# Two kept weight chunks in spare PSUM columns, read back in quarters; five ring slots, 48 resident chunks and 32-wide transposes

## The chip, the cores and the metric

One core of a Trainium2 chip runs the whole kernel. The metric is the time of one execution in device microseconds; the number that counts is the median of the runs. The profile is one execution, recorded by the hardware; "TensorE" and PE are the same engine, as are VectorE and DVE, ScalarE and ACT, GpSimd and POOL, SyncE and SP.

## The reference

Two independent parts, their outputs set side by side. Part A is a long convolution by FFT (2048 steps, 1024 channels) with a short shift filter. Part B, where the change lies, is an attention with a recurrent memory over 64 segments of 32 steps:

```python
def _A_ref(q, k, v, shift_k, ssm_k, ssm_D):
    ...                                   # kv = shifted k * v
    y = irfft2(rfft2(kv_pad) * rfft2(kf_pad))[:, :S]
    y = y + kv * ssm_D[None, None, :]
    return q * y

def _B_ref(x, mem0, Wq, Wk, Wv, Wo, seg_len):      # 32 heads of 128, M = 8 memory rows
    mem = mem0
    for s in range(n_seg):                          # 64 segments
        h = jnp.concatenate([mem, x[:, s*seg_len:(s+1)*seg_len]], axis=1)   # 40 rows
        q, k, v = h @ Wq, h @ Wk, h @ Wv            # einsum 'btd,dhe->bhte'
        scores = jnp.where(mask, q @ k^T * scale, -1e9)
        o = softmax(scores) @ v
        o = jnp.einsum('bhte,hed->btd', o, Wo)
        mem = o[:, :M, :]                           # feeds the next segment
        outs.append(o[:, M:, :])
return jnp.concatenate([a, b], axis=-1)
```

Each segment needs all four weight matrices, and its memory rows come out of the segment before.

## The kernel before

The first part of the program (up to about 392 us) computes part A and, between its stages, the keys, queries and values of the last 8 steps of every segment, which need no memory; they go to DRAM (REC for keys, queries and x, VBD for values). Up to 445 us the last of these values are computed (L765), while weights for the recurrence are placed. Then come the 64 segments, in an order written out by hand.

The weights of part B are cut into 64 chunks of 128 x 2048 bf16 (512 KB). A chunk is named by its position 0 to 63 in the order of use: 0 to 7 keys of head group 0 (the projection k0), 8 to 15 q0, 16 to 23 k1, 24 to 31 q1, 32 to 39 and 40 to 47 the values (pv0, pv1), 48 to 63 the output projection. 47 chunks stay in SBUF (tiles Wres, Wmid, Wmore, Wlate, pw). The 17 of `STREAM` are read from a DRAM copy (WS) in every segment by SP (L724) into a ring of six slots (`wring0` to `wring5`): when a chunk has been used, `done` frees its slot and `fetch` issues the next load into it. SP issues in program order, so a load that waits for its slot holds up those behind it. The slot `wring2` comes free only in segment 0, because the value stores to VBD (L768) leave from its memory.

Two of the 17 are kept in spare PSUM columns after segment 0 (`KEPT`, copied by `keep`). "A" lies in the bank of OTp and is copied back to SBUF by four DVE copies, `quarter` (L817), into the buffers tagged rot and QT; the output projection uses it in four pieces. Of "B", five eighths are kept; `fetch` loads the rest (192 KB, L721) into a ring slot and moves the kept part into the same slot by two DVE copies (`move`, L800). So a segment has 15.4 loads.

A projection (`Proj.run`, L918) takes 8 chunks; of each chunk four matmuls, 32 columns of weights wide, work side by side on four column tiles of the array. ScalarE casts the sum to SBUF (`evac`, L927, buffer rot), four 128-wide transposes (L933) turn it, and DVE or ScalarE copies the result (the first keys: L1027 on DVE; the first queries: L1031 on DVE). Between a cast and its transposes stands half a projection of other work. Scores are L939 and L942, the weighted values L980 and L984, the output projection L1002 (64-wide, two side by side). At the end of a segment ScalarE casts the result to Y (L1078, buffer PT), POOL stores Y to the output (L1080, two DMAs), and `fill_mem` transposes Y (L862, two pairs) to put the 8 memory rows into the next segment's input (L863): the first pair before any projection, the second after four chunks of k0.

The pools release a buffer when everything that read it is done, DMAs included. The tag PT is shared by Y and by PT, the softmax result; QT by the first output rows and the second queries; rot by all casts.

Of the kernel before, what the change touches and what calls it, by code (L numbers as in the profile page):

```python
# [18 lines left out]
NEG = -1.0e9  # L19


STREAM = (0, 5, 10, 15, 21, 26, 31, 36, 41, 46, 49, 52, 54, 57, 60, 61, 63)
KEPT = {14: "A", 4: "B"}
K0_ORDER = (0, 1, 4, 5, 2, 3, 6, 7)
N2, N3 = 12, 19
WO_COPY = 29
Q_LOAD = (10, 13, 16, 19)
X_LOAD = 1
RING = 6
LATE_SLOT = 4  # L30

PITCH = 2048
SCRATCH = 1024
# [383 lines left out]
def b_kernel(ctx: ExitStack, tc, x, mem0, Wq, Wk, Wv, Wo, outb, n_seg, run_a):  # L417
    nc = tc.nc
# [19 lines left out]
    streamed = set()  # L438
# [21 lines left out]
    def stream_src(ch):  # L460
        return WS[ring_order.index(ch), :, 0:2048]
# [233 lines left out]
    def more(i):  # L695
# [7 lines left out]
    kept = {order_s[i]: name for i, name in KEPT.items()}  # L703
    at_hand = {}
    loads = [(s, ch) for s in range(n_seg) for ch in order_s
             if s == 0 and ch not in v_temp[2:] or s > 0 and kept.get(ch) != "A"]
    live = {}
    now = [0]
    free = [4, 5, 0, 1, 3]
# [6 lines left out]
    def fetch():  # L716
        if loads:
            s, ch = loads.pop(0)
            live[s, ch] = k, t = slot()
            if s > 0 and ch in kept:  # L720
                nc.sync.dma_start(t[:, 0:768], stream_src(ch)[:, 0:768])  # L721
                move(kept[ch], t, True)
            else:
                nc.sync.dma_start(t[:], stream_src(ch))  # L724

    def place(ch, ap):
        res[ch] = ap
# [11 lines left out]
    with c0p:  # L739
        temps = dict(zip(v_temp, homes_v))  # L740
        wv = [group(2, 0, temps), None]
        for _ in rest:
            store()
        wv[1] = group(2, 1, temps)
        for i, ch in enumerate(v_temp):
            if i >= 2:
                home = (lambda i=i: more(i)) if i < len(v_temp) - 2 else (lambda k=i - len(v_temp) + 4: pw(k))
                at_hand[ch] = (wv[ch[2]][ch[1]], home)
        while stores:
            store()  # L750
        with tc.issue_after(got[-1].ins):
            for _ in range(2):
                fetch()
        n_k = len(own[0, 0])
        late = late[n_k:-1] + late[4:n_k] + late[:4] + late[-1:]
        for g in range(2):
            ws = wv[g]
            if g == 0:
                vsts = slot16([128, 4, 4, 512], BF, "vst")
            for tb in range(4):  # L760
                vst = vsts[:, tb] if g == 0 else pair()[:].rearrange("p (c w) -> p c w", c=4)
                for c in range(4):
                    ps = ps0.tile([128, 512], F32, tag="ps0", name="vb_ps")
                    for kc in range(8):
                        nc.tensor.matmul(ps[:], lhsT=xbt(kc)[:, 16 * tb:16 * tb + 16, :].rearrange("p s t -> p (s t)"),  # L765
                                         rhs=ws[kc][:, c * 512:(c + 1) * 512], start=(kc == 0), stop=(kc == 7))
                    evac(vst[:, c, :], ps[:])
                nc.scalar.dma_start(  # L768
                    VBD[16 * tb:16 * tb + 16, :, :, :, g * 128:(g + 1) * 128].rearrange("s t c i e -> (s t) (c i) e"),
                    vst.rearrange("p c (i e) -> p (c i) e", i=4))  # L770
            if g == 0:
                with tc.issue_after(got[-1].ins):
                    place_late(4, stage_home)
                    for i in [*range(len(v_temp) - 2, n_more), *range(len(v_temp) - 2)]:
                        place_late(1, lambda: more(i))
                    place_late(1, lambda: pw(2))
                    place_late(4, stage_home)
        assert len(late) == len(at_hand)

    one = ctx.enter_context(tc.tile_pool(name="b_one", bufs=1, side="right", reuse_waits="tile"))  # L780
# [11 lines left out]
    homes = {"B": [(OTi[:, :, 416:512], slice(384, 768)), (tpi[:, 1, :], slice(768, 1024))]}  # L792

    def move(name, t, back):
        for p, cols in homes[name]:
            w = t[:].bitcast(I32)[:, cols]
            if len(p.shape) == 3:
                w = w.rearrange("p (b x) -> p b x", b=4)
            src, dst = (p, w) if back else (w, p)
            nc.vector.tensor_scalar(out=dst, in0=src, scalar1=0, scalar2=None, op0=ALU.bitwise_or)  # L800

    def quarter_cols(q):
        return [1024 * (q // 2) + 512 * dh + 256 * (q % 2) for dh in range(2)]
# [1 line left out]
    def keep(ch):  # L805
        t = live[0, ch][1]
        if kept[ch] == "A":
            w = t[:].bitcast(I32).rearrange("p (hh dh f x) -> p hh f dh x", hh=2, dh=2, f=2)
            for q in range(4):
                nc.vector.tensor_scalar(out=OTi[:, q, 160:416].rearrange("p (dh x) -> p dh x", dh=2),  # L810
                                        in0=w[:, q // 2, q % 2], scalar1=0, scalar2=None, op0=ALU.bitwise_or)
        else:
            move(kept[ch], t, False)

    def quarter(q):
        t = one.tile([128, 512], BF, tag=("rot", "QT")[q % 2], name="quarter")
        nc.vector.tensor_scalar(out=t[:].bitcast(I32), in0=OTi[:, q, 160:416], scalar1=0, scalar2=None,  # L817
                                op0=ALU.bitwise_or)
# [15 lines left out]
    def done(ch):  # L834
        if now[0] == 0 and ch in at_hand:
            place_late(1, at_hand[ch][1])
        elif ch in streamed and (now[0] == 0 or kept.get(ch) != "A"):
# [3 lines left out]
            i = order_s.index(ch)  # L841
            if now[0] == 0 and i == LATE_SLOT:
                free.append(2)
                fetch()
            fetch()

    P_pad = one.tile([128, 5, 64], BF, name="P_pad")
# [18 lines left out]

    with tc.manual_schedule():
        for _ in range(RING - 3):
            fetch()
        load_x(0)  # L870
        Y = one.tile([128, 512], BF, tag="PT", name="Y0")
# [12 lines left out]
        for s in range(n_seg):  # L884
# [19 lines left out]
            class Proj:  # L904


                def __init__(self, m, g):
                    self.m, self.g, self.kc = m, g, 0
                    self.acc = ps_acc.tile([128, 512], F32, tag="acc", name="acc")

                def run(self, n=8):
                    for n_kc in range(self.kc, self.kc + n):
                        kc = K0_ORDER[n_kc] if (self.m, self.g) == (0, 0) else n_kc
                        ch = (self.m, kc, self.g)
                        w = pieces(ch)
                        for c in range(4):
                            for x, y, r in columns(w, 512 * c, 512 * c + 512):
                                nc.tensor.matmul(self.acc[32 * c:32 * c + 32, x - 512 * c:y - 512 * c],  # L918
                                                 lhsT=hT[:, kc, :], rhs=r, start=(n_kc == 0 and x == 512 * c),
                                                 stop=(n_kc == 7), tile_position=(0, 32 * c))  # L920
                        done(ch)
                    self.kc += n
                    return self

# [5 lines left out]
            def transposes(sb):  # L930
                tp = tps[:, 0, :]
                for i in range(4):
                    nc.tensor.transpose(tp[:, i * 128:(i + 1) * 128], sb[:, i * 128:(i + 1) * 128], ident[:])  # L933
                return tp.rearrange("p (i c r) -> p i c r", i=4, c=4)

            def scores(g, QT, KT):
# [89 lines left out]
            last_queries(0)  # L1026
            nc.vector.tensor_copy(KT0[:, :, :, 0:32], transposes(k0))  # L1027
# [125 lines left out]
```

## Time and profile before

| | |
|---|---|
| median of 3 runs | 1904.04 us (1904.03 to 1904.1) |
| profiled execution, time | 1907.36 us |
| profiled execution, span of the core | 1905.6 us |
| mean granted TensorE clock | 0.982 (1.00 in the segments) |
| bytes by DMA | 678 MB, mean 356 GB/s |
| loads of L724 | 961, and 63 partial ones of L721 |
| start of segment 1 and segment 63 | 475.81 and 1879.10 us |

The page gives for every engine its busy time in the span; the slices show when. In the segments each engine's work repeats every 22.5 us, so one segment read closely stands for all. A busy TensorE in this view can still stand still for a short time between matmuls; that is read in the timeline, from one start to the next.

### The profile page before, as it was taken

What the parts mean: (1) busy time and instruction counts of PE and PEld (TensorE: products, weight loads), DVE (VectorE), ACT (ScalarE), POOL (GpSimd) and SP (SyncE); (2) the same over time, 40 slices, a digit from 0 to 9 for tenths busy, and PEclk for the clock granted to TensorE, in tenths of its full rate; (3) what the DMA queues carried; (4) which work ended last, traced back from release to release, by engine and by line L of the source; (5) the groups of instructions that cost most, each with busy time, mean ns of one, the idle gap of its engine ahead of it and who ended that gap; (6) DMA issues with size and microseconds to landing.
All of it is one profiled execution on the core that took longest, in us unless ns stands there. A gap on an engine that the chain in (4) does not pass through costs nothing.

```text
span 1905.6 us, 62245 instructions
## 1 busy us (share of the span) xinstructions
PE 1749.0 (92%) x26353; PEld 831.1 (44%) x26353; DVE 853.8 (45%) x2812; ACT 674.8 (35%) x1195; POOL 342.8 (18%) x1014
## 2 busy tenths in 40 slices
PE   6989986778999999999999999999999999999998
PEld 3433322333444444444444444444444444444444
DVE  9927863202344444444444444444443444444443
ACT  6945640112333333333333333333333333333333
POOL 4003341000121111111121111111111111111111
PEclk9999998989999999999999999999999999999999
DMA  9989889998999999999999999999999999999998
GB/s 338 351 302 329 291 271 333 327 284 277 349 373 374 373 378 373 377 372 373 373 373 378 373 376 372 370 372 372 379 374 369 371 378 374 375 373 371 372 379 311
DMA packets 251211, 678.00 MB, mean 356 GB/s; under 512 B 74850, under 2 KB 82930, under 8 KB 250932
## 3 DMA queue, kind: packets, MB, share of 16 engines
q1 hardware_dynamic: 178692, 604.26, 85.0%
q0 software_dynamic: 17488, 46.70, 7.0%
q10 hardware_dynamic: 54752, 23.07, 4.5%
q8 instruction: 206, 3.38, 0.7%
q14 instruction: 73, 0.60, 0.1%
HBM read 618.35 MB, written 59.24 MB: 356 GB/s over the span
## 4 chain that ended last, share of the span: by engine, by line
PE 80%; DMA 7%; DVE 5%; issue 4%; ACT 2%; POOL 0%; ACTq 0%; SPq 0%; DVEq 0%; POOLq 0%
PE acc L918 38%; PE yacc L1002 22%; PE kb_ps L625 5%; PE tps L933 4%; DMA wring<-WS 3%; PE vb_ps L765 3%; DMA REC<-stage 2%; PE OTp L980 1%; ACT s_sb L243 1%; DVE rec L863 1%; PE SB L942 1%; PE tps L862 1%; PE s_ps L241 1%; DMA REC<-xt 1%; PE SB L939 1%
## 5 line engine op out<-in xcount | busy, mean ns | idle before, releaser
L918 PEld LDWEIGHTS <-rec 128*32 128x32 bf16 x12288 | 283.6, 96 | 300.2 <-DVE rec L863 60.7
L927 ACT CAST qkv_sb<-acc 128x512 bf16<-128x512 f32 x384 | 224.7, 585 | 480.0 <-PE acc L918 287.9
L1002 PEld LDWEIGHTS <-OT 128*64 128x64 bf16 x4348 | 255.1, 109 | 195.3 <-ACT OT L992 27.6
L918 PE MATMUL acc<-wring,rec 128*32 128x512 bf16 x2556 | 252.7, 382 | 22.8 <-DVE rec L863 19.1
L918 PE MATMUL acc<-Wres,rec 128*32 128x512 bf16 x3328 | 249.4, 380 | 0.6 <-issue 0.6
L1002 PE MATMUL yacc<-wring,OT 128*64 128x512 bf16 (+1 forms) x1540 | 235.9, 380 | 5.0 <-DMA wring<-WS 4.9
L918 PE MATMUL acc<-Wmid,rec 128*32 128x512 bf16 x3072 | 234.4, 382 | 0.0
L1002 PE MATMUL yacc<-Wmore,OT 128*64 128x512 bf16 (+1 forms) x1280 | 185.4, 381 | 0.0
L817 DVE TENSOR_SCALAR quarter<-OTp 128x256 int32<-128x256 int32 x252 | 101.1, 422 | 187.6 <-ACT OT L992 149.3
L1080 POOL DMA_DIRECT2D out_dram<-Y x128 | 63.7, 502 | 484.5 <-ACT Y L1078 484.2
L918 PE MATMUL acc<-pw,rec 128*32 128x512 bf16 x1796 | 144.8, 382 | 0.1
L1078 ACT CAST Y<-yacc 128x256 bf16<-128x256 f32 x128 | 41.4, 375 | 274.5 <-PE yacc L1002 274.5
L992 ACT CAST OT<-OTp 128x640 bf16<-128x640 f32 x128 | 88.6, 692 | 129.7 <-PE OTp L984 129.0
L918 PE MATMUL acc<-Wlate,rec 128*32 128x512 bf16 x1280 | 104.0, 384 | 17.1 <-DVE rec L863 17.1
L948 DVE TENSOR_REDUCE mx<-SB 128x5 f32<-128x200 f32 x128 | 47.1, 368 | 153.4 <-PE SB L942 153.3
L856 POOL DMA_DIRECT2D rec<-REC x64 | 36.2, 566 | 405.0 <-PE acc L918 372.1
L1002 PE MATMUL yacc<-Wlate,OT 128*64 128x512 bf16 x768 | 105.7, 383 | 0.2 <-ACT OT L992 0.2
L933 PEld LDWEIGHTS <-qkv_sb 128*128 128x128 bf16 x1024 | 57.8, 97 | 109.5 <-ACT qkv_sb L927 108.0
L933 PE MATMUL tps<-ident,qkv_sb 128*128 128x128 bf16 x1024 | 101.6, 222 | 0.4 <-ACT qkv_sb L927 0.3
L893 POOL COPY KT<-rec 128x128 bf16<-128x128 bf16 x128 | 38.2, 298 | 329.4 <-PE SB L942 324.2
L863 DVE COPY rec<-tps 128x32 bf16<-128x32 bf16 x128 | 22.3, 175 | 165.1 <-PE tps L862 115.8
L1027 DVE COPY KT<-tps 128x512 bf16<-128x512 bf16 x64 | 27.1, 424 | 152.2 <-PE tps L933 152.2
(215 smaller groups left out, 2392.9 us busy)
## 6 DMA issues: line engine op xcount, KB each, us to landing
wring<-WS SPq DMA_DIRECT2D x961, 512.0 KB, 6.0
rec<-REC POOLq DMA_DIRECT2D x64, 192.0 KB, 5.8
wring<-WS SPq DMA_DIRECT2D x63, 192.0 KB
SK<-s_sb SPq DMA_DIRECT2D x16, 512.0 KB, 4.8
SU<-s_sb SPq DMA_DIRECT2D x16, 512.0 KB, 4.9
Kg<-SK SPq DMA_DIRECT2D x32, 256.0 KB, 4.2
Ug<-SU SPq DMA_DIRECT2D x32, 256.0 KB, 5.7
REC<-stage ACTq DMA_DIRECT2D x16, 512.0 KB, 10.9
```

The lines of the kernel that those rows point to most:

```text
L625: nc.tensor.matmul(ps[:], lhsT=ws[kc][:, hl * 128:(hl + 1) * 128], rhs=xbt(kc).rearrange("p s t -> p (s t)"), start=(kc == 0), stop=(kc == 7))
L765: nc.tensor.matmul(ps[:], lhsT=xbt(kc)[:, 16 * tb:16 * tb + 16, :].rearrange("p s t -> p (s t)"), rhs=ws[kc][:, c * 512:(c + 1) * 512], st ...
L817: nc.vector.tensor_scalar(out=t[:].bitcast(I32), in0=OTi[:, q, 160:416], scalar1=0, scalar2=None, op0=ALU.bitwise_or)
L863: nc.vector.tensor_copy(hT.rearrange("p (dh j) t -> p dh j t", dh=2)[:, :, 2 * half:2 * half + 2, 0:NM], tp.rearrange("p (j dh r) -> p dh ...
L918: nc.tensor.matmul(self.acc[32 * c:32 * c + 32, x - 512 * c:y - 512 * c], lhsT=hT[:, kc, :], rhs=r, start=(n_kc == 0 and x == 512 * c), st ...
L927: nc.scalar.copy(sb[:], self.acc[:])
L933: nc.tensor.transpose(tp[:, i * 128:(i + 1) * 128], sb[:, i * 128:(i + 1) * 128], ident[:])
L948: nc.vector.tensor_reduce(out=mx[:], in_=S, op=ALU.max, axis=AX.X)
L992: nc.scalar.copy(OT[:], o_view)
L1002: nc.tensor.matmul(yacc[64 * dh:64 * dh + m, x - o:y - o], lhsT=lhsT, rhs=r, start=(h == 0 and x == o), stop=(h >= 30), tile_position=(0, ...
L1078: nc.scalar.copy(Y[:, 256 * half:256 * half + 256], yacc[:, 256 * half:256 * half + 256])
L1080: nc.gpsimd.dma_start(bass.AP(outb.tensor, outb.offset + SEG * s * 2048 + 512 * dh, [[2048, 32], [1, 512]]), Y[64 * dh + NM:64 * dh + 40, :])
```

## The change

`STREAM` is a new list of 16 positions; 48 chunks are resident, the 48th in `wring2`, and the ring has five slots. Both kept chunks, A (now position 61) and B (now position 20, in k1), stay in PSUM whole (the last eighth of B in an SBUF tile `B_rest`), and neither is loaded after segment 0: 14 loads a segment. B is used like A in four quarters, `quarter_b`, each copied by DVE into a work buffer (PT, QT, PT, rot) and multiplied inside k1, out of its turn in the sum. Only three chunks and two quarters now stand between q0's cast and its transposes, where four chunks stood. The copy of the first queries goes from DVE to ScalarE. All 128 x 128 transposes of the segments become four of 32 columns each, on four column tiles (`turn_tile`).

```diff
-STREAM = (0, 5, 10, 15, 21, 26, 31, 36, 41, 46, 49, 52, 54, 57, 60, 61, 63)
+STREAM = (1, 7, 13, 18, 20, 24, 30, 35, 41, 46, 49, 52, 55, 59, 61, 62)
 KEPT = {14: "A", 4: "B"}
-RING = 6
-LATE_SLOT = 4
+RING = 5
...
-             if s == 0 and ch not in v_temp[2:] or s > 0 and kept.get(ch) != "A"]
+             if s == 0 and ch not in v_temp[2:] or s > 0 and ch not in kept]
...
-            if s > 0 and ch in kept:
-                nc.sync.dma_start(t[:, 0:768], stream_src(ch)[:, 0:768])
-                move(kept[ch], t, True)
-            else:
-                nc.sync.dma_start(t[:], stream_src(ch))
+            nc.sync.dma_start(t[:], stream_src(ch))
...
+        place_late(1, lambda: base.tile([128, 2048], BF, tag="wring2", name="Wring"))
...
+    B_rest = one.tile([128, 4, 32], I32, name="B_rest")
+    B_homes = [tpi[:, 1, :].rearrange("p (c x) -> p c x", c=4),
+               SB[:].bitcast(I32)[:, 200:456].rearrange("p (c x) -> p c x", c=4),
+               OTi[:, :, 416:480], OTi[:, :, 480:512]]
+
+    def bits(dst, src):
+        nc.vector.tensor_scalar(out=dst, in0=src, scalar1=0, scalar2=None, op0=ALU.bitwise_or)
+
+    def quarter_b(q, tag):
+        n = 64 if q < 3 else 32
+        t = one.tile([128, 4, 2 * n], BF, tag=tag, name="quarter_b")
+        bits(t[:].bitcast(I32), B_homes[q])
+        w = [(512 * c + 128 * q, 512 * c + 128 * q + 2 * n, t[:, c, :]) for c in range(4)]
+        if q == 3:
+            w += [(512 * c + 448, 512 * c + 512, B_rest[:].bitcast(BF)[:, c, :]) for c in range(4)]
+        return w
...
+    def turn_tile(dst, src):
+        for e in range(0, 128, 32):
+            nc.tensor.matmul(dst[e:e + 32, :], lhsT=src[:, e:e + 32], rhs=ident[:], start=True, stop=True,
+                             is_transpose=True, tile_position=(0, e))
...
-            nc.tensor.transpose(tp[:, j * 128:(j + 1) * 128], Y[:, j * 128:(j + 1) * 128], ident[:])
+            turn_tile(tp[:, j * 128:(j + 1) * 128], Y[:, j * 128:(j + 1) * 128])
...
-        for _ in range(RING - 3):
+        for _ in range(RING - 2):
             fetch()
...
+                def add(self, kc, w, start=False, stop=False):
+                    for c in range(4):
+                        for x, y, r in columns(w, 512 * c, 512 * c + 512):
+                            nc.tensor.matmul(self.acc[32 * c:32 * c + 32, x - 512 * c:y - 512 * c],
+                                             lhsT=hT[:, kc, :], rhs=r, start=start and x == 512 * c,
+                                             stop=stop, tile_position=(0, 32 * c))
...
-                    nc.tensor.transpose(tp[:, i * 128:(i + 1) * 128], sb[:, i * 128:(i + 1) * 128], ident[:])
+                    turn_tile(tp[:, i * 128:(i + 1) * 128], sb[:, i * 128:(i + 1) * 128])
...
-            k1 = Proj(0, 1).run(4)
+            k1 = Proj(0, 1)
+            if s > 0:
+                kb = [ch[1] for ch in kept if kept[ch] == "B"][0]
+                b0, b1 = quarter_b(0, "PT"), quarter_b(1, "QT")
+                k1.run(1)
+                k1.add(kb, b0)
+                b2 = quarter_b(2, "PT")
+                k1.run(2)
+                k1.add(kb, b1)
+            else:
+                k1.run(4)
             QT0 = one.tile([128, 4, 4, 32], BF, tag="QT", name="QT")
-            nc.vector.tensor_copy(QT0[:], transposes(q0))
-            k1 = k1.run(4).evac()
+            nc.scalar.copy(QT0[:], transposes(q0))
+            if s > 0:
+                b3 = quarter_b(3, "rot")
+                k1.run(3)
+                k1.add(kb, b2)
+                k1.add(kb, b3)
+            k1 = k1.run(8 - k1.kc).evac()
```

More of the change, by code (lines that the diff above doesn't have):

```diff
@@ L791, in b_kernel @@
     OTi, tpi = OTp[:].bitcast(I32), tps[:].bitcast(I32)
[L792 to L800, printed above, removed]
+    B_rest = one.tile([128, 4, 32], I32, name="B_rest")
[12 more added lines that the diff above has]
+        return w
     def quarter_cols(q):
@@ L809, in keep @@
             for q in range(4):
-                nc.vector.tensor_scalar(out=OTi[:, q, 160:416].rearrange("p (dh x) -> p dh x", dh=2),
-                                        in0=w[:, q // 2, q % 2], scalar1=0, scalar2=None, op0=ALU.bitwise_or)
-        else:
-            move(kept[ch], t, False)
+                bits(OTi[:, q, 160:416].rearrange("p (dh x) -> p dh x", dh=2), w[:, q // 2, q % 2])
+        else:
+            w = t[:].bitcast(I32).rearrange("p (c f x) -> p f c x", c=4, f=4)
+            for q in range(3):
+                bits(B_homes[q], w[:, q])
+            bits(B_homes[3], w[:, 3, :, 0:32])
+            bits(B_rest[:], w[:, 3, :, 32:64])
     def quarter(q):
         t = one.tile([128, 512], BF, tag=("rot", "QT")[q % 2], name="quarter")
-        nc.vector.tensor_scalar(out=t[:].bitcast(I32), in0=OTi[:, q, 160:416], scalar1=0, scalar2=None,
-                                op0=ALU.bitwise_or)
+        bits(t[:].bitcast(I32), OTi[:, q, 160:416])
         return [(o, o + 256, t[:, 256 * dh:256 * dh + 256]) for dh, o in enumerate(quarter_cols(q))]
@@ L836, in done @@
             place_late(1, at_hand[ch][1])
-        elif ch in streamed and (now[0] == 0 or kept.get(ch) != "A"):
+        elif ch in streamed and (now[0] == 0 or ch not in kept):
             if now[0] == 0 and ch in kept:
@@ L840, in done @@
             free.append(live.pop((now[0], ch))[0])
[L841 to L844, printed above, removed]
             fetch()
@@ L914, in run @@
                         ch = (self.m, kc, self.g)
[L915 to L921, printed above, removed]
+                        if s == 0 or ch not in kept:
+                            self.add(kc, pieces(ch), n_kc == 0, n_kc == 7)
+                            done(ch)
                     self.kc += n
```

## The prediction

> **What bounds the kernel now.** I read the page's busy rows first, then the windows of single segments, then the chain, then the timeline around one transpose, then the landings of the output store. The page, busy us of each engine:
>
> ```profile
> PE 1749.0 (92%) x26353; PEld 831.1 (44%) x26353; DVE 853.8 (45%) x2812; ACT 674.8 (35%) x1195; POOL 342.8 (18%) x1014
> ```
>
> The windows (stretch, its length, busy us of each engine with its count, granted clock, DMA share, GB/s):
>
> ```profile
> 800.00:822.52 22.52, 21.46 (x392) 10.64 (x388) 9.51 (x36) 7.45 (x15) 3.87 (x14) 1.00 1.01 381
> 450.00:455.00 5.00, 5.00 (x112) 2.54 (x108) 2.59 (x7) 1.83 (x3) 0.90 (x5) 1.00 1.05 408
> ```
>
> A segment of the recurrence takes 22.52 us at full clock; TensorE (PE) is busy for 21.46 of them, and the DMA share reads 1.01. So there are two candidates for the bound. The chain decides. From 475.81 us to the end its longest pieces are these, and there are only five of this kind:
>
> ```profile
> 945.32 7.86 DMA wring<-WS
> 1171.45 7.56 DMA wring<-WS
> ...
> 1757.82 7.56 DMA wring<-WS
> ```
>
> Segment starts (the first L862 transpose of each) lie 22.51 to 22.52 us apart in most segments. The 62 intervals from 475.81 to 1879.10 sum to 1403.3 us, 7.0 more than 62 x 22.52: 2.8 in the first, 4.2 in all others. So TensorE's own order is the bound, and late loads cost 7 us altogether. Also, 1.01 is not the end of the queue: 450 to 455 us shows 408 GB/s where a segment needs 381. Cutting traffic alone is worth 7 us at most; the rest must come from TensorE.
>
> TensorE's order at one transpose (start, us, engine, line, operation, out<-in, count):
>
> ```profile
> 820.16 0.58 ACT L927 CAST qkv_sb<-acc 128x512 bf16<-128x512 f32 x1 [3.06 <-issue]
> 820.54 0.39 PE L918 MATMUL acc<-Wmid,rec 128*32 128x512 bf16 x4
> 820.86 0.40 PE L933 MATMUL tps<-ident,qkv_sb 128*128 128x128 bf16 x4
> 821.19 0.61 PE L918 MATMUL acc<-Wmid,rec 128*32 128x512 bf16 x8
> 821.29 0.42 DVE L1027 COPY KT<-tps 128x512 bf16<-128x512 bf16 x1 [2.33 <-PE tps L933]
> 821.63 0.39 PE L918 MATMUL acc<-Wlate,rec 128*32 128x512 bf16 x4
> ```
>
> Four 32-wide projection matmuls run side by side; a chunk takes 0.216 us (821.63 to the next at 821.85). The chunk of 820.54 therefore leaves the array at 820.755, but the first transpose starts at 820.86: 0.105 idle. The four transposes start 0.056 apart (820.86, 820.93, 820.98, 821.04 in the trace), so they end at 821.095, and the next chunk starts at 821.19: 0.09 idle. The block takes 0.43 us for 0.22 of streaming. Between 32-wide projections and 32-wide scores (L939) there is no such gap.
>
> **The change, part by part.**
>
> *32-wide transposes.* Each 128-wide transpose becomes four 32-wide ones side by side, the shape of the projections. If they overlap like projections, streaming stays 4 x 0.056 and both gaps go: 0.215 less for each of the four L933 blocks. But the first gap also hid a wait on ScalarE. From a projection's last matmul start to the end of its cast is 0.494 + 0.58 (821.85 to 822.34, then 0.58), and 0.06 to reach PE: 1.13 us. With four chunks between, PE arrives after 0.216 x 5 = 1.08, so 0.05 of the gain is lost at k0 and q1 (0.16 each is left). At k1 the scores lie between: all 0.215. At q0 the change puts only three chunks and two quarters between: 0.216 + 3 x 0.216 + 2 x 0.056 = 0.98, so PE waits 0.16 and 0.05 is left. The second L862 pair loses its 0.11 gap; the first waits for Y anyway: 0. Sum: 0.16 + 0.05 + 0.215 + 0.16 + 0.11 = 0.695 us a segment.
>
> *Quarters of chunk B on PE.* Four groups of 128 columns and the last split in two of 64, instead of one chunk of 512: 4 x 0.056 against 0.216, so 0.01. The nearest rows agree on both sides: the 256-wide quarter pairs of A take 0.11 (813.73 to 813.84), the 40-wide score groups start 0.025 apart. A rule speaks against this: the Trainium skill, TensorEngine Tiling (Array Packing), section Instruction Overhead, gives every matmul about 60 cycles and warns against tiling what is already small. Taken as serial cost, an estimate from that page is 16 more matmuls x 0.025 us (60 columns' worth of a 0.216 us chunk) = 0.4 us a segment, and the sum would be 25 us worse; the score groups show 0.006 per matmul.
>
> *Copies on VectorE (DVE).* Removed: two copies back (0.56 + 0.41, L800) and the Q copy (0.42), which goes to ScalarE at 0.58 behind q0's cast and before k1's; scores come 1.2 us after it, 1.05 is needed: 0. Added: three copies of 0.42 like L817 and one half as wide, about 0.28. The first starts when the K copy ends, 0.84 after the k0 transposes start, is done at 1.27 and wanted at 0.224 + 0.864 + 0.216 = 1.30: just in time. The last one overwrites the buffer that the q0 transposes read: 0.42 + 0.28 + 0.06 = 0.76 after their start, wanted at 0.71: 0.05.
>
> *The new wait.* The first copy goes into the buffer tagged PT, last used by Y, so it waits until both output stores of the segment before have landed. Behind it on DVE stand the other three copies and the softmax; PE waits for all of them. Today PT's next writer comes about 9 us later. The stores are issued 0.52 and 1.02 us after the segment starts (at 816.87), as the timeline has it:
>
> ```profile
> 817.39 1.00 POOL L1080 DMA_DIRECT2D out_dram<-Y  x2 [7.34 <-ACT Y L1078]
> ```
>
> The store's own view, from 700 to 1800 us and for the last segment (duration of the issue in ns; time from issue to landing):
>
> ```profile
> L1080 POOL DMA_DIRECT2D out_dram<-Y x98: 496/502/509, 704.8 to 1790.0; - x98
> ...
> DMA to landing us min/median/max: 4.2/4.8/5.8
> ...
> L1080 POOL DMA_DIRECT2D out_dram<-Y x2: 496/496/496, 1902.1 to 1902.6; - x2
> ...
> DMA to landing us min/median/max: 1.7/1.7/1.8
> ```
>
> Call L the time from the first issue to the second landing: 5.3 today, 2.2 in the last segment, where no loads run. B's first quarter is wanted 5.2 us after the segment starts; landing, copy and two hand-overs end at 0.52 + L + 0.53. The wait is L - 4.15, of which 0.1 replaces the wait at q0. Bounds: 0 at L = 2.2, 1.05 at 5.3. What L follows is the loads in flight at the issue: counted from the DMA packets, 3.1 today and none at the end. After the change the slots freed shortly before are those of positions 59 and 62, at -2.2 and -0.9 us, and no load is cut short; with the 1.2 us from issue to first packet and 1.25 per load that is 1.5 to 1.8 in flight. L grew by 3.1 us for 3.1 loads, 1 us each, so it should be 3.7 to 4.0, nearer to the last segment's end than to today's; with the scatter of 0.5 above I take 0.03. A rule would settle it: the Trainium skill, DMA: Bandwidth & Descriptors, section Queues, rings and completion order, says that an engine round-robins between rings packet by packet; then a store would hardly feel the loads and the wait would be 0. The rows above, 1.7 against 4.8, contradict it.
>
> *Fourteen loads, five slots.* 15.4 chunks of 524 KB fall to 14: 8.37 to 7.65 MB a segment, 349 GB/s at 21.9 us. Loads land after a median of 6.0 us (4.8 to 7.9). From slot free to next use there are now 7.1 to 8.6 us; by the new positions 6.2 to 8.3, the tightest being 52, 49 and 35. These are issued where loads landed after 5.5 to 5.9. Cost 0.02; of today's 7 us, 5 come back.
>
> *Segment 0.* The 48th chunk goes to wring2, whose last user is the VBD store of L768, issued at 445.8. It is needed as the fifth chunk, at 447.0. That store takes 15.0 us beside ten loads; with five, I count about 9, then 3.5 for the chunk: PE stops until about 458. SyncE (SP) holds the next loads behind it, but all five slots are full by then. Today segment 0 takes 30.0 us from 445.8, with 7.5 of waits at 463 to 475. New: 1.2 + 11 + 20.8 + 1 = 34: 4 us more (0 to 9). The stages before: one copy to WS less, no other step on the chain, 0 +- 2.
>
> **Sum.** A segment: -0.695 + 0.01 + 0.05 + 0.03 + 0.02 = -0.585, so 21.93 us. Times 63: -36.9. Stalls -5, segment 0 +4: -37.9. The profiled execution took 1907.36 us (span 1905.6, 1.8 around it): 1869.5. The median of the runs, 1904.04, lies 3.3 below it: 1866. Own range: gains of 0.45 to 0.72 a segment and the bounds of segment 0 and the stalls give 1852 to 1882.
>
> **Rivals.**
> 1. *The store holds B's first quarter.* If L stays at 5.3, each segment pays 1.05 more: 22.95 us, +27 for 63, +4 in segment 0, -5 of stalls: 1930. It turns slower from L of about 4.85. For: 4.2 to 5.8 in every segment today. Against: half the loads in flight, and a waiting PE lets the queue empty. 0.17.
> 2. *Five slots starve.* If loads at the tight places took 7.7, PE would wait 1.3 us a segment: about 1948. Against: 9% fewer bytes. 0.08.
> 3. *Transposes do not overlap.* Sixteen in a row take 0.9 us instead of 0.22: +2.7 for four blocks, +0.6 for the fills: about 2075. Against: the projections overlap in this shape. 0.08.
> 4. *Nothing to gain*: other waits take up the gaps, 1897 to 1910: 0.07.
>
> **Numbers.** Forecast 0.60. The range 1850 to 1930 leaves out rivals 2 in part and 3 and the tails. Faster by over 0.2% (which is about what a measurement can tell): the forecast, some of 1, 2 and 4: 0.73; same 0.05; slower 0.22.
>
> **What would show it.** Right: segments 21.8 to 22.0 apart; L918 to L862/L933 without a gap; a wait of about 0.15 at q0's transposes; quarter_b's first copy waiting little or not on out_dram; one stop of about 11 us on Wring in segment 0. Wrong: DVE idle on out_dram for 1 us a segment, PE on wring, or 0.05 between single transposes.

## The result, and the profile after

The changed kernel takes 1968.1 us (median, 1960.52 to 1976.29) against 1904.07 us for the kernel before on the same chip: a ratio of 1.0331, 95% interval 1.0286 to 1.0376. It is slower; the forecast was 1866, faster. The profiled execution took 1969.65 us, with a span of 1967.8.

The page of the changed kernel, its busy row, the queue that brings instructions (packets, MB, share), and the chain by engine:

```profile
PE 1719.1 (87%) x31169; PEld 872.0 (44%) x31201; DVE 864.5 (44%) x2877; ACT 709.0 (36%) x1259; POOL 344.9 (18%) x1013
...
q8 instruction: 244, 4.00, 0.8%
...
PE 67%; DMA 18%; DVE 4%; ACT 4%; issue 4%; POOL 2%; ACTq 1%; DVEq 0%; another core or an unknown queue 0%; POOLq 0%; SPq 0%
```

TensorE (PE) has less to do, 1719 us instead of 1749, although it has more matmuls. But it no longer works through: 87% of the span instead of 92%. The windows show it in one stretch of 22.5 us:

```profile
1000.00:1022.50 22.50, 19.78 (x436) 10.67 (x436) 9.49 (x36) 7.98 (x15) 2.71 (x12) 1.00 0.88 314
```

PE is busy for 19.78 us of it, the DMA share is 0.88. So neither TensorE's work nor the bandwidth sets the time, and the clock is full (1.00). Over 62 segments a segment takes 23.52 us on average, 22.63 before, and 21.93 in the forecast. The waits of PE between 500 and 1840 us (who waited, for whom: us in total, times, longest) name the two things in between:

```profile
PE acc L920 <- DVE quarter_b L794: 53.2, 57, 2.2
...
PE acc L920 <- issue: 7.2, 11, 1.3
PE OTp L989 <- issue: 3.7, 6, 1.2
```

The first row is the wait for B's first quarter, in nearly every segment. The rows with "issue" are stops in which PE waited for no semaphore; with the smaller ones they sum to 14.5 us here. In the same view of the kernel before all of them come to 0.6 us. The timeline shows the one stop of segment 0, and then one segment in which the wait is long:

```profile
458.52 0.62 PE L920 MATMUL acc<-Wring,rec 128*32 128x512 bf16 x4 [12.06 <-DMA Wring<-in_B_Wk_dram]
...
998.67 1.02 POOL L1104 DMA_DIRECT2D out_dram<-Y  x2 [7.33 <-ACT Y L1102]
...
1002.01 0.41 PE L862 MATMUL tps<-ident,qkv_sb 128*32 128x128 bf16 x16
1002.24 0.39 PE L920 MATMUL acc<-Wmid,rec 128*32 128x512 bf16 x4
...
1004.97 0.42 DVE L794 TENSOR_SCALAR quarter_b<-tps 128x256 int32<-128x256 int32 x1 [2.08 <-DMA out_dram<-Y]
...
1005.45 0.24 PE L920 MATMUL acc<-quarter_b,rec 128*32 128x128 bf16 x4 [1.95 <-DVE quarter_b L794]
```

Sixteen narrow transposes start at 1002.01, and the next chunk at 1002.24: 0.23 us for the block that took 0.33 and a gap of 0.1 before it. That part of the change works. Then DVE stands 2.08 us until the output store has landed, and PE 1.95 us until the copy is there. The store's own view, from 500 to 1900 us:

```profile
DVE quarter_b L794: 49.9, 48
...
DMA to landing us min/median/max: 3.5/4.7/5.9
```

48 copies waited for it. A store lands after 4.7 us, 4.8 before: the relief that the forecast counted on isn't there.

### The profile page after: what moved, and what is told of

It is laid out like the page before. It is cut to its first block, busy times and chain, and to the rows that moved or that the text cites. A ratio compares the mean times of both kernels' runs of the same rounds, so it can differ in the third digit from the quotient of the medians.

```text
span 1967.8 us, 71785 instructions
## 1 busy us (share of the span) xinstructions
PE 1719.1 (87%) x31169; PEld 872.0 (44%) x31201; DVE 864.5 (44%) x2877; ACT 709.0 (36%) x1259; POOL 344.9 (18%) x1013
## 4 chain that ended last, share of the span: by engine, by line
PE 67%; DMA 18%; DVE 4%; ACT 4%; issue 4%; POOL 2%; ACTq 1%; DVEq 0%; another core or an unknown queue 0%; POOLq 0%; SPq 0%
PE acc L920 26%; PE yacc L1011 23%; DMA out_dram<-Y 13%; PE kb_ps L624 4%; PE tps L862 3%; PE vb_ps L760 3%; DMA REC<-stage 2%; PE OTp L989 1%; DVE quarter_b L794 1%; POOL out_dram L1104 1%; ACT Y L1102 1%; ACT s_sb L242 1%; PE SB L951 1%; PE s_ps L240 1%; PE SB L948 1%
## 5 line engine op out<-in xcount | busy, mean ns | idle before, releaser
L920 PEld LDWEIGHTS <-rec 128*32 128x32 bf16 x13296 | 321.7, 96 | 368.3 <-issue 108.7
L920 PE MATMUL acc<-Wres,rec 128*32 128x512 bf16 x3328 | 254.9, 380 | 5.9 <-issue 5.1
L920 PE MATMUL acc<-Wmid,rec 128*32 128x512 bf16 x3072 | 247.7, 381 | 0.0
L920 PE MATMUL acc<-wring,rec 128*32 128x512 bf16 x2304 | 232.6, 381 | 1.5 <-issue 1.4
L1011 PE MATMUL yacc<-Wmore,OT 128*64 128x512 bf16 x1536 | 210.5, 381 | 0.1
L1011 PE MATMUL yacc<-wring,OT 128*64 128x512 bf16 (+1 forms) x1284 | 196.9, 379 | 3.1 <-DMA wring<-WS 2.7
L920 PE MATMUL acc<-Wlate,rec 128*32 128x512 bf16 x1280 | 115.3, 385 | 22.1 <-DVE rec L869 21.2
L920 PE MATMUL acc<-quarter_b,rec 128*32 128x128 bf16 x1008 | 58.1, 216 | 58.6 <-DVE quarter_b L794 58.4
L862 PE MATMUL tps<-ident,qkv_sb 128*32 128x128 bf16 x4096 | 106.1, 220 | 1.9 <-issue 1.7
L862 PEld LDWEIGHTS <-qkv_sb 128*32 128x32 bf16 x4096 | 71.9, 96 | 65.0 <-ACT qkv_sb L936 45.4
```

The source lines that it names most:

```text
L862: nc.tensor.matmul(dst[e:e + 32, :], lhsT=src[:, e:e + 32], rhs=ident[:], start=True, stop=True, is_transpose=True, tile_position=(0, e))
L1011: nc.tensor.matmul(yacc[64 * dh:64 * dh + m, x - o:y - o], lhsT=lhsT, rhs=r, start=(h == 0 and x == o), stop=(h >= 30), tile_position=(0, ...
```

## The experiments

The theory after this result had two costs that add up: the wait for the store, about 1.0 us a segment (the forecast's first rival), and the stops without a semaphore, about 0.5. The other candidates were the narrow transposes themselves, the five slots and the quarters. Each time is compared with the kernel before on the same chip.

**Another buffer for the first quarter.**

```
-                b0, b1 = quarter_b(0, "PT"), quarter_b(1, "QT")
+                b0, b1 = quarter_b(0, "E"), quarter_b(1, "QT")
```

> The changed kernel, but the first quarter of chunk B is copied into the buffer tagged E (softmax scratch, idle then) and not into PT, so that it does not wait for the output store of Y. Theory: two losses, the wait for the store (first quarter multiplied 6.3 us after the segment starts, where 5.2 was expected; about 1.0 us a segment) and PE stops of about 0.5 us a segment between instructions that wait for no semaphore. Taking away the first gives 63 x 0.95 = 60 us: 1905 to 1920, with segments 22.3 to 22.8 us apart, and the PE stops stay. Rival (five slots and a later DMA are the bound, the wait for the store only shows it): the wait moves to wring, 1945 or more.

Measured: 1961.73 us, ratio 1.0292 [1.0264, 1.032]. The wait is all but gone from the trace (2.6 us in 7 waits): the first quarter's matmul comes 5.17 us after the segment's start (6.3 on average with the store). But the time hardly moved (1905 to 1920 was expected), because the stops without a semaphore took its place. PE's waits, 500 to 1840 us:

```profile
PE tps L862 <- issue: 19.4, 21, 1.7
PE acc L920 <- issue: 15.7, 18, 1.7
PE SB L951 <- issue: 7.3, 9, 1.6
```

All "issue" rows together are 51.4 us here, against 14.5 with the wait in place. The rival's 1945 or more holds as a number only, since PE waits 0.3 us in all for a ring load. The stops had been named before this run; that they would grow when the wait goes was in no theory.

**The transposes 128 wide again, all else changed.**

```
-        for e in range(0, 128, 32):
-            nc.tensor.matmul(dst[e:e + 32, :], lhsT=src[:, e:e + 32], ... tile_position=(0, e))
+        nc.tensor.transpose(dst, src, ident[:])
```

> The changed kernel with 128-wide transposes again, all else as changed. Theory (the PE stops come from the supply of PE instructions, of which the 32-wide transposes add 120 a segment): the stops of 0.5 us a segment go, the two gaps of 0.2 us behind B's first quarter come back, those ahead of it lie in the wait for the store: 1950 to 1970. Rival (the number of instructions does not matter, the gaps do): about 0.4 us a segment more, 1990 or above.

Measured: 1959.95 us, 1.0285 [1.0259, 1.031]. This is what the theory expected: the stops without a semaphore are gone (0.7 us in all), the wait for the quarter stays (32 us in 46 waits over the run). The interval overlaps that of the whole change (1.0286 to 1.0376), so the narrow transposes bring the change nothing that shows.

**The narrow transposes alone, in the kernel before** (`turn_tile` of the change in place of both transposes).

> The kernel before with the 32-wide transposes alone. By the prediction's term, 0.695 us a segment less: 63 x 0.695 = 44 us, 1860, if nothing else comes up. Theory (instruction supply): 96 pairs more a segment give some PE stops, 0.2 to 0.4 us a segment, so 1870 to 1885. Rival (the transposes gain nothing, or the loads become the bound at 8.4 MB a segment): 1895 or above, with PE waiting on wring.

Measured: 1954.06 us, 1.0259 [1.0231, 1.0287]: the part that was to bring the gain makes the kernel slower by itself. The theory had expected far less of the stops (1870 to 1885); the rival's 1895 or above came, but not its cause, since PE waits 0.5 us in all for the ring. PE's waits, 500 to 1840 us:

```profile
PE acc L923 <- issue: 24.8, 27, 2.3
PE tps L861 <- issue: 13.6, 12, 1.9
PE SB L947 <- issue: 8.6, 9, 1.7
```

In all 60.4 us of "issue" rows. They count idle time only from the modelled end of the matmul before; from one start to the next, compared with the same instructions in the run with half the loads below, the stops take 93 us over 62 segments, 1.5 each. Two neighbouring stops in the timeline:

```profile
1004.36 0.38 PE L1007 MATMUL yacc<-wring,OT 128*64 128x512 bf16 x1 [0.93 <-issue]
...
1019.86 0.19 PE L947 MATMUL SB<-KT,QBm 128*32 128x40 bf16 x1 [0.76 <-issue]
```

They fall into the middle of a group: one matmul of four runs, the next of the same shape doesn't. Counting PE's instructions between such stops (weight loads, matmuls, semaphore instructions, in the order of the program), I found distances of 255, 768, 769, 255, 1537, 1023, 769 and 1023 between the first nine: multiples of 256 within one. All 64 stops of this window lie at the same place of the count modulo 256, within one. The trace also has 16 KB packets on the queue named "instruction" (4.00 MB in 244 packets in the page above, 64 bytes for each of 256 instructions). After a stop, PE resumes 1.2 to 1.6 us after the end of such a packet. So PE stops for its instructions, 256 at a time.

**As many more instructions, where PE idles.** 64 load-and-matmul pairs of 8 columns in each segment of the kernel before, half ahead of the first transposes and half behind them; they alter the sums in the score bank.

> The kernel before with 64 more pairs of weight load and matmul a segment (32 wide, 8 columns each, into unused PSUM columns), half just ahead of the first transposes of Y and half just behind them, where PE stands idle for about 0.5 us each time. They do not take PE time from the path. Theory (supply of PE instructions): 128 instructions more a segment make PE stop elsewhere, 0.2 to 0.6 us a segment: 1915 to 1945, and the stops end soon after an instruction packet of 16 KB. Rival (stops come from loads or from the ring): no change, 1904 within 3 us.

Measured: 1905.95 us, 1.0014 [1.0001, 1.0027], with 0.9 us of "issue" rows. The theory on record (stops elsewhere, 1915 to 1945) was wrong; the number is the rival's, which blamed loads or the ring. Where PE idles, the number of instructions costs next to nothing by itself. That left the theory that the runs below test: a block of 256 instructions has to be brought while the 256 before it run; that takes 5 to 6 us beside the weight loads, and PE stops where the 256 run in less. What counts is how dense the instructions lie, and how busy the DMA engines are.

**Both edits together: E buffer and 128-wide transposes.**

> The changed kernel with B's first quarter copied into the E buffer and the transposes 128 wide again: neither of the two stops is left. Theory (two costs that stand in for one another: the copy that waits for the Y stores, and TensorE stopped for its instructions where 256 of them are run in less than the 5 to 6 us that their fetch takes): both go at once, first quarter at 5.2 us after the segment's start, a segment of about 22.4 to 22.6 us (22.0 at the least stretches, and the 0.5 of instruction stops that the kernel before had room for), segment 1 starts at about 482; time 1900 to 1912. Rival (the chunk copied in quarters costs by itself, by DVE and by 5 slots, whatever the two): 1935 or more, as either edit alone gave (1962 and 1960).

Measured: 1921.48 us, 1.0099 [1.0082, 1.0116]. The two costs do stand in for one another: either edit alone left 1960, both together take away 40 us. A wait for the store gives the instruction fetch its time, and a stop for instructions gives the store its time. The number expected, 1900 to 1912, was missed by 9 us: a segment takes 22.62 us at the median, 22.74 on average, and the kernel before 22.52 and 22.63. Keeping B in quarters costs 0.1 us a segment even so, and segment 0 has become longer (segment 1 starts at 483.10 instead of 475.81).

**The same number of extra instructions, in the dense stretch** (16 pairs ahead of each group of scores and behind the transposes of k1 and q1; `start=False`, into columns that nobody reads).

> The kernel before with 64 more load-and-matmul pairs of 8 columns in each segment, as many as in the run that put them where TensorE idles (1906), but 16 each ahead of the two groups of scores and behind the transposes of k1 and q1, so in the stretch of 7 to 13 us of the segment; they add into columns of the score bank that nobody reads. Theory (instructions are fetched 256 at a time and a fetch takes 5 to 6 us): the pairs' own time of 0.4 us a segment, and stops of 0.5 to 1.2 us a segment at multiples of 256 instructions; 1950 to 2000, with stops between instructions that wait for no semaphore. Rival (the place does not matter, only the pairs' own time): 0.2 to 0.4 us a segment, 1918 to 1930, no such stops.

Measured: 2005.49 us, 1.0524 [1.05, 1.0548], 5 us above the theory's range; a segment takes 24.07 us on average and 23.35 at the least. The same 64 pairs cost 2 us where PE idles and 100 us here, though not by stops alone. PE's waits, 500 to 1840 us:

```profile
PE SB L1023 <- DVE SB L880: 16.2, 54, 0.3
PE acc L918 <- issue: 11.1, 16, 1.5
```

The first row is a cost that I had not put in: the pairs ahead of the second scores wait for DVE's writing of the score bank, 0.3 us a segment. The "issue" rows are 26.9 us together. So the number supports the theory, but less purely than I expected it to: 0.84 of the 1.56 us a segment is own time and this wait (the shortest segment against 22.51), and the stops at multiples of 256 instructions take 0.70 (43 us over 62 segments, from one start to the next).

**Narrow transposes, half the bytes loaded.**

```
-                nc.sync.dma_start(t[:], stream_src(ch))
+                w = 1024 if s > 0 else 2048
+                nc.sync.dma_start(t[:, 0:w], stream_src(ch)[:, 0:w])
```

with the left half of each streamed chunk used for both halves.

> The kernel before with 32-wide transposes (1954) and, from segment 1 on, only the left half of each streamed chunk loaded and used for both halves (B's kept chunk as before), so that the ring loads move half of their bytes; the output is that of other weights. Theory (a fetch of 256 instructions is slow because the weight loads lie on the same DMA engines): a fetch comes down to 3 to 4 us, the stops go, and the narrow transposes' gain shows: 1855 to 1890. Rival (fetches are slow by themselves, or the stops are in TensorE's own sequencer): the stops stay, 1940 to 1955.

Measured: 1854.71 us, 0.9745 [0.9731, 0.976]: exactly the same PE instructions as in the narrow transposes alone, and 99 us less. PE's waits, 500 to 1840 us, the largest of the "issue" rows, 0.5 us in all where full loads had 60.4:

```profile
PE SB L948 <- issue: 0.3, 1, 0.3
PE OTp L989 <- issue: 0.2, 1, 0.2
```

Nearly every segment takes the shortest time, 21.74 us. So it isn't PE's own dispatch that stops it, but the loads beside which the instructions travel. The halved loads come in packets of 2 KB where the full ones have 4 KB; whether it is the bytes or the size of the packets, no run here tells apart.

The traces allow a sum. In a segment of this run 256 consecutive instructions (128 pairs of load and matmul, from start to start) take 4.17 us at the least, about 4.2 from 3 to 9 us after the segment's start, and over 8 in the output projection. If a fetch takes T and PE stops for T minus the time of the 256, then T = 5.25 us gives stops of 1.5 us a segment with full loads (measured: 23.26 on average against 21.74) and 0.1 for the kernel before, whose densest 256 take 4.76 us (measured: 0.03 at multiples of 256). T is a fit, but the instruction packets give a reading beside it. With full loads the packet for a block ends 3.8 us (median, 1.9 to 5.9) after the block before it has begun; 1.0 of this is the packet's own time, and at a stop PE goes on 1.4 later: 5.2 together. With half the loads it ends after 2.1, of which 1.0 is again its own time: 3.5 together, less than the 4.17 that the 256 take. So the loads delay the packet's start and do not stretch the packet.

**Narrow only where instructions are sparse, in the changed kernel** (E buffer; 32-wide for the second half of the memory columns and k0; the chunk that PE waited 12 us for exchanged with one of the output projection).

> The changed kernel with the E buffer, 32-wide transposes only for the second half of the memory columns and for k0 (the first 3 us of a segment), 128-wide elsewhere, and the chunk that TensorE waited 12 us for in segment 0 exchanged with an output-projection chunk used later. Theory: against the run with the E buffer and 128-wide transposes alone, 0.16 to 0.27 us a segment less (10 to 17 us in all) and 6 us less in segment 0: 1880 to 1895, below the kernel before. Rival (each pair added costs its instructions' fetch somewhere in the segment, whichever place it has): 1900 to 1915.

Measured: 1908.44 us, 1.0031 [1.0015, 1.0047], short of the 1880 to 1895 expected and inside the rival's range. The shortest segment, 22.35 us, has the gain; the average, 22.74, has lost it. With the quarters a segment has 838 PE instructions, and its densest 256 take 4.27 us: the quarters' 32 small instructions lie in the same stretch. Exchanging the chunk removed the stop at Wring, but PE then stopped 5.84 us for a ring load at 462 us; segment 0 became 4 us shorter, not 6.

**The changed kernel, half the bytes loaded.**

> The changed kernel with, from segment 1 on, only the left half of each streamed chunk loaded and used for both halves (the output is that of other weights). Theory (all that the forecast missed is the two stops, and both come from the weight loads on the DMA engines): the store pair lands about half a microsecond sooner and holds the first quarter by 0 to 0.4 us a segment, a fetch of 256 instructions takes under 4.1 us and stops nothing much; a segment of 21.9 to 22.2 us beside segment 0's 482: 1862 to 1885, where the forecast was 1866. Rival (the quarters, or 5 slots and 14 loads, cost something else as well): 1895 or more.

Measured: 1880.09 us, 0.9873 [0.9855, 0.989], as the theory had it. One segment in the windows, and the store's landing from 500 to 1800 us:

```profile
992.03:1014.03 22.00, 20.92 (x460) 11.11 (x460) 9.58 (x37) 7.96 (x16) 3.89 (x14) 1.00 0.58 184
```

```profile
DMA to landing us min/median/max: 1.7/2.3/3.9
```

Against the window of the changed kernel PE is back to work, at a DMA share of 0.58. The store lands in 2.3 us instead of 4.7, and the wait for the quarter all but vanishes (1.1 us over 1340). Both stops are gone, and the segment is 22.07 us on average: 1.45 of the 1.59 us by which the forecast missed.

**The kernel before, half the bytes loaded.**

> The kernel before with the same halved loads, as the measure for the run with narrow transposes and halved loads (1854.7). Theory: the kernel before loses only 0.1 us a segment to stops for instructions and some 5 us to loads in all, so 1893 to 1901, and the narrow transposes are worth 40 to 46 us (0.65 to 0.74 us a segment) where no fetch stops them. Rival (the halved loads help in ways that have nothing to do with instructions): below 1885.

Measured: 1901.71 us, 0.9985 [0.9973, 0.9997], just above what was expected. Halving the traffic of the kernel before is worth next to nothing, as the prediction said. Beside it, the narrow transposes' 1854.71 are worth 47 us, 0.77 us a segment (22.51 to 21.74).

**Sparse narrow transposes, in the kernel before.**

```
+            turn_tile(tp[:, j * 128:(j + 1) * 128], Y[...], (128, 32)[half])
...
+            nc.vector.tensor_copy(KT0[:, :, :, 0:32], transposes(k0, 32))
```

> The kernel before with 32-wide transposes only for the second half of the memory columns and for k0; q0, k1, q1 stay 128 wide. Theory, with the times of the 256-instruction stretches read from the traces and a fetch of 5.25 us: these two give 0.24 us a segment, and stops stay at 0.1 (all narrow: 0.76 gained, 1.5 lost; measured for that 1954): 1887 to 1893, faster than both kernels. Rival (a transpose's own pairs cost a fetch wherever they are): 1900 to 1906.

Measured: 1892.93 us (1891.91 to 1895.56), 0.9945 [0.9929, 0.9961], at the upper end of the expected range: faster than both kernels. Two neighbouring segments in the timeline, at their first and second pair of transposes:

```profile
1013.66 0.28 PE L861 MATMUL tps<-ident,Y 128*128 128x128 bf16 x2 [0.47 <-ACT Y L1086]
1015.14 0.28 PE L864 MATMUL tps<-ident,Y 128*32 128x128 bf16 x8
...
1035.92 0.29 PE L861 MATMUL tps<-ident,Y 128*128 128x128 bf16 x2 [0.46 <-ACT Y L1086]
1037.40 0.28 PE L864 MATMUL tps<-ident,Y 128*32 128x128 bf16 x8
```

They start 22.26 us apart instead of 22.51; "issue" rows are 2.6 us from 500 to 1840. Two of the six places take a third of the gain and little of the cost.

**The rest in 64-wide pieces** (q0, k1 and q1, on top of the last edit).

> As the run before this one, with q0, k1 and q1 transposed in 64-wide pieces, two load-and-matmul pairs for each block instead of one or four. Theory: half of the gain of the 32-wide ones (0.27 us a segment), and 24 more instructions in the dense stretch, which at a fetch of 5.25 us make 0.3 us of stops more: 1885 to 1897. Rival (64-wide pieces do not overlap, so nothing is gained): 1900 to 1910.

Measured: 1904.96 us, 1.0011 [0.9998, 1.0023], the rival's range. The shortest segment is 22.30 us, no shorter than with these three 128 wide (22.25): the 64-wide pieces gained nothing, and by the medians the gain of the other two went as well. The timeline of this run has a 32-wide block and a 64-wide one, each with the chunk behind it:

```profile
1021.12 0.41 PE L864 MATMUL tps<-ident,qkv_sb 128*32 128x128 bf16 x16
1021.35 0.60 PE L926 MATMUL acc<-Wmid,rec 128*32 128x512 bf16 x8
...
1023.18 0.41 PE L864 MATMUL tps<-ident,qkv_sb 128*64 128x128 bf16 x8
1023.53 0.40 PE L926 MATMUL acc<-Wmid,rec 128*32 128x512 bf16 x4
```

The rival's reason does not hold: the 64-wide pieces run two at a time, one pair 0.056 us behind the other, as the four 128-wide ones do. But the chunk behind them starts 0.35 us after the first, as with 128-wide ones (0.33), where it is 0.23 with 32-wide ones, and the gap ahead stays too. In these traces the gaps go only where the transposes are as wide as the matmuls around them; why a change of width makes a gap was not tried.

## Why the prediction was wrong

By its own steps, in us a segment:

- **32-wide transposes, -0.695: right where nothing stops them.** -0.77 with the loads halved on both sides, in the kernel before, for which the same working, with 0.16 left at q0, gives -0.805. They overlap, and rival 3 is out.
- **What was not in the sum: the instructions themselves.** Each narrow block has 24 more, and the sum counted only the time of their streaming. That is the step that failed most. With full loads it costs 1.5 us a segment by itself, twice the gain; in the changed kernel, where the store's wait gives part of the time, 0.5 (32 us over 62 segments, from one start to the next). The rows to see it in were there: the instruction queue in the page and PE's order of instructions. The kernel before has 770 PE instructions a segment and runs its densest 256 in 4.76 us, with 0.03 us of stops; the change has 922, and runs its densest 256 in 3.5. The kernel before stood at the edge of this limit, and hardly showed it.
- **The new wait, +0.03: mis-sized, about 1.0** (58.4 us over 62 segments by the waits of the whole run, 67 from one start to the next, against the run with half the loads). The formula L - 4.15 was right: the first quarter is wanted at 5.2, and came at 5.17 once it had its own buffer. What failed is L: averaged over the segments it is 5.15 us (5.5 in the kernel before), where the sum had 3.7 to 4.0. Both steps to it were off. Counted as loads issued whose last packet is still to come, 2.9 are in flight at the first issue and 3.8 in the kernel before, 0.9 fewer where the sum had 1.3 to 1.6 fewer; the level depends on how one counts. And with these 0.9 the last store packet comes 0.5 us sooner (4.84 to 4.35 after the first issue), not 1 us for each load: the slope was drawn from one far point, the last segment's end with no loads. Rival 1 had the mechanism and, for itself, the price of 1.05; it missed the rest. Halving the loads brings the landing to 2.3 us, so it is the weight loads that make it late; by which turn in the queues, no run here shows.
- **Quarters and last copy, +0.06: too small.** With the loads halved, a segment takes 22.02 us with quarters and five slots and 21.74 without: 0.28. The sum has 0.17 of it: the 0.06, and 0.11 as q0's gain that it cut from 0.16 to 0.05. The last copy makes the difference. In the run of the changed kernel with halved loads it starts 0.53 us after q0's transposes, where the sum had 0.42, so that by the sum's own working it is there at 0.53 + 0.29 + 0.06 = 0.88, wanted at 0.71, and costs 0.17 instead of 0.05 (PE's matmuls of the fourth quarter start 0.21 us behind the third's, 0.15 more than streaming needs). DVE's timeline:

```profile
1020.43 0.29 DVE L795 TENSOR_SCALAR quarter_b<-OTp 128x128 int32<-128x128 int32 x1 [0.53 <-PE tps L866]
```

- **Fourteen loads, five slots: right, as far as tested.** Loads land after 5.5 us instead of 6.0, and the waits for ring loads are 0.9 us between 500 and 1840, and 0.2 with both edits, in segments of 22.62 us. At the 21.9 us of the forecast no run had full loads. Rival 2 is out at these paces. Rival 4 had other waits take up the gaps, and they did, but it named none, and priced them at a gain of nothing instead of a loss of 64 us.
- **Segment 0, +4: 6.5.** Segment 1 starts at 482.33 instead of 475.81. The stop on Wring came where it was put (until 458.5), and a ring load held PE for 1.7 us. What the sum left out is TensorE's clock. The windows show it at 0.50 behind the stop, and in the kernel before across the start of segment 1:

```profile
458.50:461.60 3.10, 3.08 (x32) 1.38 (x35) 0.00 (x0) 0.59 (x1) 0.00 (x0) 0.50 0.10 13
...
472.60:482.60 10.00, 8.33 (x61) 2.41 (x61) 0.94 (x4) 1.23 (x3) 2.42 (x8) 0.50 0.95 370
```

At 0.50 a chunk takes 0.43 us (479.42 to 479.85 in the kernel before) instead of 0.216. So about 1.5 us of the changed kernel's segment 0 is lost behind the stop. It also accounts for the first interval of the kernel before, 25.35 us, in which PE waits for no load: the prediction put the 2.8 us there down to late loads.

Together: 21.93 us, +0.1 for the quarters, +1.0 for the store, +0.5 for instructions gives 23.5; measured 23.52.

The two surprises hide one another. Taking either away brought 6 to 8 us, no more than the scatter of the runs (1960 to 1976), both together 47, with the narrow transposes' gain given up. An experiment that removes one suspect and sees no change has not acquitted it.

The Trainium skill, Runtime: NRT & Kernel Launch, section Instruction fetch mechanics, has the shape of the limit: instructions come in blocks of 16 KiB, 256 of them, through a DMA queue of the engine's own, the next while the current one runs. It calls the cost of a boundary "mostly hidden". The first half agrees with this case's packets and distances; the second does not hold here, where the boundaries cost 1.5 us a segment in the run with the narrow transposes alone.

## What to carry to other kernels

Before cutting a TensorE operation into smaller ones, count instructions as well as columns: take from the trace the shortest time in which 256 consecutive PE instructions run, and see whether the cut brings it under the fetch time (some 5 us here beside 330 to 375 GB/s of traffic). Spend extra instructions where the engine idles or streams long rows. And when a copy's buffer was last read by a store, its landing belongs to the path: measure how it moves with the traffic that will be there, not between today's and none, and before dropping a suspect, remove it together with its rival.

## What the runs showed of the hardware

- Stops of TensorE for its instructions: PE stands in the middle of a group, at multiples of 256 instructions, 60 us over 1340 (by the "issue" rows) with the instructions of narrow transposes and 363 GB/s of traffic, 0.5 us with the same instructions at 207 GB/s.
- The same 64 pairs of instructions a segment cost 2 us in PE's idle time and 100 us in its dense stretch; of the 100, some 43 are stops at multiples of 256, the rest the pairs' own time and a wait for DVE.
- A 32 KB output store lands in 4.7 to 5.1 us beside full weight loads (the two kernels and the narrow transposes alone), 2.3 to 2.9 beside half of them, 1.7 beside none (the last segment's).
- 32-wide transposes between 32-wide matmuls overlap without gaps, sixteen in 0.23 us; 64-wide pieces keep the gaps of 128-wide ones and brought nothing.
- The granted TensorE clock was 0.50 for 3.1 us of work behind a stop of 12 us, and a chunk takes 0.43 us at 0.50 instead of 0.216.

Open: what in the loads, bytes or packets, delays the start of an instruction packet, and why a change of width makes a gap.
